# A hand-written order of two cycles for the score matmuls of an attention and Fourier-mixing kernel

## The chip, the cores and the metric

The kernel runs on one core of a Trainium2 chip. The metric is the device time of one execution in microseconds (us), the median of several runs. One further execution was taken with the hardware profiler; its page and its trace are what is read here. The engines are named as the profile names them: PE is TensorE's matmul, PEld its weight load, DVE is VectorE, ACT is ScalarE, POOL is GpSimd, SP is SyncE (here it only issues DMAs).

## The reference

Two token mixers over the same input are blended by a gate. x has 2048 rows of 640; there are 32 heads of 20.

```python
def reference(A_x, A_wqkv, A_wo, B_x, B_dft_seq_re, B_dft_seq_im, B_dft_hid_re, B_dft_hid_im, gate_w):
    def _A_ref(x, wqkv, wo):
        ...
        scores = jnp.einsum("bhqd,bhkd->bhqk", q, k) * (Dh ** -0.5)
        p = _softmax(scores, axis=-1)
        o = jnp.einsum("bhqk,bhkd->bhqd", p, v)
        return (lambda x, *d: x.transpose(*d))(o, 0, 2, 1, 3).reshape(B, S, D) @ wo

    def _B_ref(x, dft_seq_re, dft_seq_im, dft_hid_re, dft_hid_im):
        a = jnp.einsum("bsd,ed->bse", x, dft_hid_re)
        b = jnp.einsum("bsd,ed->bse", x, dft_hid_im)
        y = jnp.einsum("ts,bse->bte", dft_seq_re, a) - jnp.einsum("ts,bse->bte", dft_seq_im, b)
        return y

    x = A_x
    g = _sigmoid((x * gate_w).sum(-1, keepdims=True))
    a = _A_ref(x, A_wqkv, A_wo)
    b = _B_ref(x, B_dft_seq_re, B_dft_seq_im, B_dft_hid_re, B_dft_hid_im)
    return g * a + (1 - g) * b
```

## The kernel before

**The stages.** First come the projections: q and k for all heads (stored to DRAM as a high and a low part), v, the gate and the first ten tiles of the DFT along the hidden axis. The long middle is one loop over 1024 steps, in which attention and the rest of the DFT share PE. Then the attention output is multiplied by wo and added to the DFT's result. The middle lasts from about 274 to 1936 us of the profiled execution, and the change lies in it.

**Attention in steps.** A unit is a pair of heads and half of the queries: 32 units of 32 steps. In a step `i` of unit `n`, the scores of 128 keys and 512 queries are computed for each of the two heads, one head from partitions 0 on (the upper half of the PE array, rows 0 to 63), the other from partition 64 on (the lower half). Each is one matmul (line 638) into a PSUM bank, and ACT takes the exponential from that bank into half of the tile `p` (line 641, "the exponential"). The softmax's maximum is not computed on the fly: it is found beforehand, by a second set of score matmuls with queries and keys exchanged (line 151), from whose banks DVE reduces the maximum (line 153). These "maxima" run LEAD = 41 steps ahead of the exponentials. When a unit's maxima are done, `s_end` reduces them to one per query (line 159) and `max_chain` transposes them on PE into a bank (line 179), splits them in two parts on DVE and has SP write them as two extra rows of q, with four DMAs. So the later exponential's matmul has 62 rows and subtracts the maximum by itself.

**Banks.** Score matmuls of both kinds and the transpose take their PSUM bank from `bank()` (line 104), which goes round five banks. So a score can start only when the score five before it has been read, by ACT if it was an exponential's, by DVE if it was a maximum's. Two more banks (`yp0`, `yp1`) belong to the DFT, one (`av`) to the product with v.

**A cycle of four steps.** A step issues, by `mixed(0)` and `mixed(1)`, an exponential's matmul of one head and a maximum's matmul of the other, so that both halves of the array work at once. After each pair comes a place for DFT work, `fill(i, z)`. A fill is one `next(fills)`: a pair of matmuls with 320 columns, one for each half (line 510; line 287 in the hidden stage). At the end of each fourth step, the last place is taken by a burst instead (line 651): `run_extras` (reads of finished DFT tiles by ACT and DVE, `finish_y` on DVE, and POOL's preparations), and `av_step` for two key tiles, 8 matmul calls of 512 columns (line 435; the profile shows 16 instructions), which use the whole array. With e for an exponential's matmul, m for a maximum's, F for a place for fills and B for the burst, a cycle is

```
em F em F em F em F em F em F em F em B
```

eight e, eight m, seven places. The 54 first cycles carry the rest of the hidden DFT, one tile of 15 fills each. From the 58th on come the 56 units of the sequence DFT, 48 fills each, spread over three or four cycles (lines 601 to 609), which makes 16 or 12 fills in a cycle. The last ten cycles have no maxima left.

**The step's other work.** `later` holds functions by the step at which they are to be issued (DMAs of SP and POOL for the next heads, for statistics, stores); the loop runs them at the start of each step. `now[0]` is the current step. The tiles `p` have five buffers; a burst frees those of four steps.

Of the kernel before, what the change touches and what calls it, by code (L numbers as in the profile page):

```python
# [12 lines left out]
AF = mybir.ActivationFunctionType  # L13
# [5 lines left out]
P = 128  # L19
# [3 lines left out]
DH = 20  # L23
ND = D // P
NS = S // P
NP = H // 2
HE = D // 2
VW = 2 * (DH + 1)
KROWS = 3 * DH
NU = 2 * NP  # L30
BW = HE + 2
LEAD = 41
HEAD = 10

# [16 lines left out]
def f32(ap):  # L51
    return ap.bitcast(F32)
# [3 lines left out]
def mix_kernel(ctx: ExitStack, tc: tile.TileContext, xa, wqk, wb, cdft, wo, out):  # L56
    nc = tc.nc
    pe, act, dve, pool, sp = nc.tensor, nc.scalar, nc.vector, nc.gpsimd, nc.sync
    ctx.enter_context(tc.manual_schedule())

    def pools(**kw):
        return ctx.enter_context(tc.tile_pool(**kw))
# [19 lines left out]
    kst = [const.tile([P, S], R, name=f"kst{i}") for i in range(2)]  # L82
# [21 lines left out]
    def bank():  # L104
        return ps_w.tile([P, 512], F32, name=f"ps{next(turn) % 5}")

    def pair_tile():
        return work.tile([P, 2, 512], F32, name="p", bufs=5)

    def raw_tile():  # L110
        return work.tile([P, 1024], F32, name="raw", bufs=3)
# [7 lines left out]
    def load_stack(p):  # L119
        kt, qt = kst[p % 2], qst[p % 2]  # L120
        u = S // 2
        for t, o, two, one, cs in ((kt, D, 0, 2, slice(0, S)), (qt, 0, 1, 0, slice(0, u)), (qt, 0, 1, 0, slice(u, S))):
            for h in range(2):
                r = (2 * p + h) * DH
                b = 64 * h
                rows = slice(o + r, o + r + DH)
                yield f32(t[b + two * DH : b + (two + 2) * DH, cs]), qk_scr[:, rows, cs]
                yield f32(t[b + one * DH : b + (one + 1) * DH, cs]), qk_scr[0, rows, cs]

    def q_unit(n):  # L130
        u = n % 2 * (S // 2)
        return qst[n // 2 % 2][:, u : u + S // 2]

    mx, nms = {}, {}
    now, later = [-1], {}

    def at_step(i, fn):
        later.setdefault(i, []).append(fn)


    def s_mm(i, h):
        n, s = divmod(i, 32)
        if n >= NU:
            return lambda: None
        qt, kc = divmod(s, 4)
        q, k = q_unit(n), kst[(n // 2) % 2]
        if n not in mx:
            mx[n] = small.tile([P, 2, 8, 4], F32, name="mx", bufs=2)
        ps = bank()
        b = 64 * h  # L150
        pe.matmul(ps, q[b : b + KROWS, qt * P : (qt + 1) * P],  # L151
                  k[b : b + KROWS, kc * 512 : (kc + 1) * 512], start=True, stop=True)
        return lambda: dve.tensor_reduce(mx[n][:, h, qt, kc : kc + 1], ps, axis=AX.X, op=ALU.max)  # L153

    def s_end(i):
        n, s = divmod(i, 32)
        if n < NU and s == 31:
            nms[n] = small.tile([P, 16], F32, name="nm", bufs=2)
            dve.tensor_reduce(nms[n], mx.pop(n).rearrange("p h q c -> p (h q) c"), axis=AX.X, op=ALU.max, negate=True)
        if s == 1 and 0 < n <= NU:  # L160
            max_chain(n - 1)
# [14 lines left out]
    def max_chain(n):  # L176
        q = q_unit(n)
        pt = bank()[:16, :P]
        pe.transpose(pt, nms.pop(n), ident)
        m1 = small.tile([16, P], R, name="m1", bufs=2)  # L180
        m2 = small.tile([16, P], R, name="m2", bufs=2)
        split(m1, m2, pt, dve, dve)

        def rows():
            for h in range(2):
                b = 64 * h + KROWS
                sp.dma_start(f32(q[b : b + 1, :]), f32(m1[8 * h : 8 * h + 8, :]))
                sp.dma_start(f32(q[b + 1 : b + 2, :]), f32(m2[8 * h : 8 * h + 8, :]))

        if now[0] < 0:  # L190
            rows()
        else:
            at_step(now[0] + 2, rows)
# [27 lines left out]
    def load_wb(j, e1=act, e2=dve):  # L221
        raws = []
        for d in range(0, ND, 3):
            n = min(3, ND - d)
            raw = raw_tile()[:, : n * BW].rearrange("p (d c) -> p d c", d=n)
            sp.dma_start(raw, wb[j, :, d : d + n])
            raws.append((d, n, raw))

        def finish():
            w = proj.tile([P, 2, ND, BW], R, name="wb", bufs=2)  # L230
            for d, n, raw in raws:
                split(w[:, 0, d : d + n], w[:, 1, d : d + n], raw, e1, e2)
            wt["b", j] = w
# [5 lines left out]
    def flush(keep=0):  # L239
        while len(stores) > keep:  # L240
            sp.dma_start(*stores.pop(0))
# [118 lines left out]
    for n, c in enumerate(order):  # L360
        for t in range(4):
            m = 4 * n + t
# [4 lines left out]
            if t == 1:  # L367
                fin()
                if n + 2 < len(order):
                    fin = load_wqk(order[n + 2])  # L370
    run_s(LEAD)
    flush()
# [17 lines left out]
    cparts, vts, pts = {}, {}, {}  # L390
# [38 lines left out]
    def av_step(i, n, kt):  # L429
        v = vts[n // 2]  # L430
        pp = [pts.pop((n, kt, qc)) for qc in range(2)]
        for qc in range(2):
            for h in range(2):
                j = 2 * qc + h
                pe.matmul(av[32 * j : 32 * j + DH + 1, :], v[:, kt, h * (DH + 1) : (h + 1) * (DH + 1)],  # L435
                          pp[qc][:, h, :], start=kt == 0, stop=kt == NS - 1)
        if kt == NS - 1:
            unit_end(i, n)
# [111 lines left out]
    def run_extras(g, most):  # L550
        while extras and most and extras[0][0] <= now[0]:
            extras.pop(0)[1]()
            most -= 1
        if more(g):
            n = g // (HT * NS) + 1
            preps.append(load_a(n, made.setdefault(n, 0)))
            made[n] += 1
        if len(preps) > 2 or preps and not more(g):
            preps.pop(0)()
# [8 lines left out]
    def start_dft():  # L568
        flush()
        proj.release()  # L570
        apool.append(pools(name="apool", bufs=1))
# [13 lines left out]
    total = 32 * NU  # L585
    done = 0
    goals, fins = {}, {}
# [4 lines left out]
    HID = 4 * NS - HEAD  # L592
# [4 lines left out]
    start = 4 * HID  # L597
    HIDS = HID * 3 * ND
# [4 lines left out]
    cycles += [(edge[u], edge[u + 1], 3 * NS) for u in range(UNITS)]  # L603
    at_goal = 0
    for c0, c1, count in cycles:
        slots = [(4 * c + k, z) for c in range(c0, c1) for k in (1, 2, 3, 4) for z in range(2 - k // 4)]
        for f, slot in enumerate(slots):
            goals[slot] = at_goal + count * (f + 1) // len(slots)
        at_goal += count

    def fill(i, z):
        nonlocal done
        while done < goals.get((i, z), 0):
            next(fills)
            done += 1

    for i in range(total + 1):
        now[0] = i
        n, s = divmod(i, 32)
        for fn in later.pop(i, ()):  # L620
            fn()
        if s % 2 == 0:
            flush()
        if i < total:
            kt, qc = divmod(s, 2)
            if s == 0 and n % 2 == 0:
                p = n // 2
                if p + 1 < NP:
                    at_step(i + 6, functools.partial(load_v, p + 1))
                    for j, args in enumerate(load_stack(p + 1)):  # L630
                        at_step(i + 2 + 2 * j, functools.partial(pool.dma_start, *args))
            q, k = q_unit(n), kst[(n // 2) % 2]
            pp = pts[n, kt, qc] = pair_tile()

            def mixed(h):
                b = 64 * h
                pt = bank()
                pe.matmul(pt, k[b : b + KROWS + 2, kt * P : (kt + 1) * P],  # L638
                          q[b : b + KROWS + 2, qc * 512 : (qc + 1) * 512], start=True, stop=True)
                most = s_mm(i + LEAD, 1 - h)  # L640
                act.activation(pp[:, h], pt, AF.Exp, scale=float(DH) ** -0.5)  # L641
                most()

            mixed(0)
            fill(i, 0)
            mixed(1)
            s_end(i + LEAD)
        if start + 2 <= i < start + 2 + HT:
            for k in range(2):
                at_step(i + 3, load_a(0, 2 * (i - start - 2) + k))  # L650
        if i and i % 4 == 0:
            run_extras(max(done - HIDS, 0) // 3, 2)
            j = i // 2 - 2
            for kt in (j, j + 1):
                av_step(i, kt // NS, kt % NS)
        else:
            fill(i, 1)
        if i % 4 == 2:
            c = i // 4
            if c + HEAD in (NS, 2 * NS):  # L660
                load_wb(3 + (c + HEAD) // NS, pool, pool)()
            if c in (HID - 5, HID - 3):
                load_c((c - HID + 5) // 2)()
            if c == HID + 1:
                cfin.append(load_c(2))
        if i == start:
            start_dft()
        if total - 10 <= i < total - 4 and i % 2 == 0:
            tt = (i - total + 10) // 2
            fins[tt] = load_o(tt)  # L670
        if i == total - 3:
            fins[0]()
    assert done == at_goal
    now[0] = total + 4
    run_extras(2 * NS * UNITS, 99)
# [70 lines left out]
```

## Time and profile before

| | us |
|---|---|
| median of 3 runs | 2012.11 (2010.03 to 2013.65) |
| the profiled execution, its own time | 2012.72 |
| its span, first to last instruction | 2011.0 |
| granted TensorE clock, mean | 0.997 of full |
| middle, first burst to last burst | 281.8 to 1935.7 |

| Group of instructions | count | busy us | mean ns |
|---|---|---|---|
| maximum, DVE line 153 | 2048 | 1262.2 | 683 |
| exponential, ACT line 641 | 2048 | 1122.6 | 598 |
| maxima's score matmul, PE line 151 | 2048 | 926.1 | 460 |
| exponentials' score matmul, PE line 638 | 2048 | 823.9 | 409 |
| DFT fill, PE line 510 | 5376 | 734.0 | 309 |
| product with v, PE line 435 | 4096 | 494.7 | 599 |

A line of the timeline gives the start in us from the span's start, how long the group of like instructions lasted, the engine, the line, the operation, the tiles (out<-in), the shapes and how many there were; in brackets stands how long the engine was idle before it and what ended that. PE's times overlap: a matmul's duration runs from its start to its result, and those of the two halves of the array run side by side. A number such as 529/550/2671 is the shortest, the median and the longest of a group, in ns.

### The profile page before, as it was taken

How to read it: one execution, taken by the hardware profiler on the slowest of the kernel's cores; microseconds unless marked ns; L12 is line 12 of the kernel's file. 1: busy time of each engine (PE TensorE's matmuls, PEld its weight loads, DVE VectorE, ACT ScalarE, POOL GpSimd, SP SyncE). 2: the span in 40 equal slices, each digit the busy share in tenths (PEclk: the TensorE clock that was granted, in tenths of full speed). 3: DMA queues.
4: the chain of work that ended last, by engine and by line, in shares of the span. 5: the costliest groups of instructions: out<-in, count | busy, mean ns of one | idle time of the engine just before them, and what ended most of it. 6: DMA issues, size and time to landing. Idle time of an engine off the chain costs nothing. (4 is left out here: it accounts for less than half of the span.)

```text
span 2011.0 us, 44080 instructions
## 1 busy us (share of the span) xinstructions
PE 1974.8 (98%) x17080; PEld 1397.7 (70%) x17080; DVE 1501.9 (75%) x2516; ACT 1253.3 (62%) x2337; POOL 986.6 (49%) x898
## 2 busy tenths in 40 slices
PE   8999999999999999999999999999999999999999
PEld 7987767666675666666666666666666666666679
DVE  3144568878887888888888888888888888888423
ACT  4221147777776666677666666766766676667751
POOL 1210001111006888556368876974775689576510
PEclk9999999999999999999999999999999999999999
DMA  6653321313125475435266736563555556444345
GB/s 218 168 166 132 128 90 45 83 50 82 35 60 161 143 204 159 118 100 153 93 169 194 207 133 194 175 184 100 165 149 145 163 171 200 131 149 144 95 150 184
DMA packets 196514, 281.05 MB, mean 140 GB/s; under 512 B 73372, under 2 KB 137916, under 8 KB 194384
## 3 DMA queue, kind: packets, MB, share of 16 engines
q1 hardware_dynamic: 158992, 246.20, 39.6%
q0 software_dynamic: 37312, 32.03, 6.4%
q8 instruction: 134, 2.20, 0.5%
q14 instruction: 76, 0.62, 0.1%
HBM read 213.81 MB, written 63.70 MB: 138 GB/s over the span
## 5 line engine op out<-in xcount | busy, mean ns | idle before, releaser
L153 DVE TENSOR_REDUCE mx<-ps 128x1 f32<-128x512 f32 x2048 | 1262.2, 683 | 233.8 <-PE ps L151 230.1
L641 ACT ACTIVATE p<-ps 128x512 f32<-128x512 f32 x2048 | 1122.6, 598 | 446.0 <-PE ps L151 354.6
L151 PE MATMUL ps<-kst,qst 60*128 60x512 f32 x2048 | 926.1, 460 | 8.0 <-ACT p L641 3.7
L638 PE MATMUL ps<-qst,kst 62*128 62x512 f32 x2048 | 823.9, 409 | 9.0 <-DVE mx L153 7.6
L510 PE MATMUL yp<-a,part 64*128 64x320 f32 x5376 | 734.0, 309 | 0.1
L510 PEld LDWEIGHTS yp<-a,part 64*128 64x128 f32 x5376 | 596.6, 187 | 23.9 <-DVE m L530 0.3
L638 PEld LDWEIGHTS ps<-qst,kst 62*128 62x128 f32 x2048 | 376.9, 185 | 235.9 <-DVE mx L153 66.9
L435 PE MATMUL av<-p,v 128*21 128x512 f32 x4096 | 494.7, 599 | 0.1
L151 PEld LDWEIGHTS ps<-kst,qst 60*128 60x128 f32 x2048 | 372.0, 184 | 59.5 <-ACT p L641 27.7
L95 POOL TENSOR_TENSOR part<-raw,part 128x1024 fp32r<-128x1024 f32 x112 | 267.1, 2385 | 9.0
L435 PEld LDWEIGHTS av<-p,v 128*21 128x21 f32 x4096 | 98.8, 100 | 226.8 <-issue 219.8
L287 PE MATMUL yp<-wb,xs 64*128 64x320 f32 x1920 | 238.1, 308 | 0.4 <-ACT raw L295 0.3
L94 POOL CAST part<-raw 128x1024 fp32r<-128x1024 f32 x112 | 116.8, 1043 | 205.2 <-PE yp L510 198.6
L406 POOL TENSOR_TENSOR raw<-raw,raw 128x1024 f32<-128x1024 f32 x78 | 188.3, 2414 | 50.1 <-DMA raw<-in_cdft 39.6
L287 PEld LDWEIGHTS yp<-wb,xs 64*128 64x128 f32 x1920 | 205.7, 187 | 9.1 <-ACT raw L295 0.6
L467 POOL TENSOR_TENSOR o<-o,rb 128x512 f32<-128x512 f32 x32 | 41.6, 1300 | 160.7 <-DMA rb<-r_scr 130.0
L94 POOL CAST wb<-raw 128x966 fp32r<-128x966 f32 (+1 forms) x4 | 3.4, 856 | 229.7 <-PE av L435 195.5
L95 POOL TENSOR_TENSOR a<-araw,a 128x320 fp32r<-128x320 f32 x112 | 98.1, 876 | 9.0
L95 DVE TENSOR_TENSOR p<-ps,p 128x512 fp32r<-128x512 f32 x40 | 27.5, 691 | 94.2 <-ACT p L92 94.2
L98 PE MATMUL ps<-xs,part 128*128 128x512 f32 x200 | 80.7, 403 | 9.1 <-ACT xs L92 7.5
L92 ACT ACTIVATE p<-ps 128x512 fp32r<-128x512 f32 x40 | 23.7, 597 | 101.5 <-PE ps L100 101.5
L420 POOL TENSOR_TENSOR araw<-araw 128x320 f32<-128x320 f32 x80 | 71.4, 892 | 20.4 <-DMA araw<-a_scr 19.9
(67 smaller groups left out, 1339.0 us busy)
## 6 DMA issues: line engine op xcount, KB each, us to landing
raw<-in_cdft SPq DMA_DIRECT2D x192, 512.0 KB
araw<-a_scr SPq DMA_DIRECT2D x192, 160.0 KB
qk_scr<-p SPq DMA_DIRECT2D x40, 512.0 KB
y_scr<-yt SPq DMA_DIRECT2D x96, 160.0 KB
kst<-qk_scr POOLq DMA_DIRECT2D x32, 320.0 KB, 12.2
qst<-qk_scr POOLq DMA_DIRECT2D x64, 160.0 KB, 8.8
a_scr<-raw SPq DMA_DIRECT2D x64, 160.0 KB
yt<-y_scr SPq DMA_DIRECT2D x64, 160.0 KB
```

The lines of the kernel that those rows point to most:

```text
L94: e1.tensor_copy(dst1, src)
L95: e2.tensor_tensor(dst2, src, f32(dst1), op=ALU.subtract)
L98: pe.matmul(ps, st1, mv1, start=first, stop=False)
L151: pe.matmul(ps, q[b : b + KROWS, qt * P : (qt + 1) * P], k[b : b + KROWS, kc * 512 : (kc + 1) * 512], start=True, stop=True)
L153: return lambda: dve.tensor_reduce(mx[n][:, h, qt, kc : kc + 1], ps, axis=AX.X, op=ALU.max)
L287: pe.matmul(yp[h][:, :HE], xs[r, xz, d, cs], w[r, wz, d, :HE], start=d == 0 and z == 0, stop=d == ND - 1 and z == 2)
L406: pool.tensor_tensor(raws[0], raws[0], raws[1], op=ALU.add if PRODUCTS[n][0][1][0] > 0 else ALU.subtract)
L420: pool.tensor_tensor(raws[0], raws[0], raws[1], op=ALU.add if PRODUCTS[n][1][1][0] > 0 else ALU.subtract)
L435: pe.matmul(av[32 * j : 32 * j + DH + 1, :], v[:, kt, h * (DH + 1) : (h + 1) * (DH + 1)], pp[qc][:, h, :], start=kt == 0, stop=kt == NS - 1)
L510: pe.matmul(yp[h][:, :HE], c[r, cz, cs], a[r, az], start=s == 0 and z == 0, stop=s == NS - 1 and z == 2)
L638: pe.matmul(pt, k[b : b + KROWS + 2, kt * P : (kt + 1) * P], q[b : b + KROWS + 2, qc * 512 : (qc + 1) * 512], start=True, stop=True)
L641: act.activation(pp[:, h], pt, AF.Exp, scale=float(DH) ** -0.5)
```

## The change

The loop over steps with its fixed pairs is replaced by a loop over cycles that follows a string. `ORDER` has one string for even and one for odd cycles; each letter issues one score (`e`, `m`), one place of fills (`F`) or the burst (`B`). Four scores (`emme`) are issued ahead of the first cycle. `heads` counts the scores of each kind; `FIRST` says, for each of eight steps, which head (and so which half of the array) comes first. Even cycles have eight e, seven m and eleven places, odd cycles eight e, nine m and seventeen places. A cycle keeps its number of fills; they are spread over its places evenly (`goals`). What a step did besides its scores is in `begin(i)`, before the step's first e, and `end(i)`, after its second; the burst has `run_extras`, `av_step` and `start_dft`. The blank lines that the diff adds are left out here.

```diff
--- before.py
+++ after.py
@@ -29,6 +29,13 @@
 KROWS = 3 * DH
 NU = 2 * NP
 BW = HE + 2
+ORDER = ("emmeFFFFmeFFemFFmeFFemFeemB", "ememmFFFFFeFmFemFFFeeFFmmFFFFFeemmB")
+FIRST = {"e": (1, 1, 1, 0, 0, 1, 1, 0), "m": (0, 0, 0, 0, 0, 0, 0, 1)}
 LEAD = 41
 HEAD = 10
@@ -603,58 +610,39 @@
     cycles += [(edge[u], edge[u + 1], 3 * NS) for u in range(UNITS)]
     at_goal = 0
     for c0, c1, count in cycles:
-        slots = [(4 * c + k, z) for c in range(c0, c1) for k in (1, 2, 3, 4) for z in range(2 - k // 4)]
-        for f, slot in enumerate(slots):
-            goals[slot] = at_goal + count * (f + 1) // len(slots)
-        at_goal += count
-
-    def fill(i, z):
+        for c in range(c0, c1):
+            share = count * (c + 1 - c0) // (c1 - c0) - count * (c - c0) // (c1 - c0)
+            places = ORDER[c % 2].count("F")
+            goals[c] = [at_goal + share * (f + 1) // places for f in range(places)]
+            at_goal += share
+    def fill(c):
         nonlocal done
-        while done < goals.get((i, z), 0):
+        goal = goals[c].pop(0) if c in goals else 0
+        while done < goal:
             next(fills)
             done += 1
-    for i in range(total + 1):
+    def begin(i):
         now[0] = i
         n, s = divmod(i, 32)
         for fn in later.pop(i, ()):
             fn()
         if s % 2 == 0:
             flush()
+        if s == 0 and n % 2 == 0:
+            p = n // 2
+            if p + 1 < NP:
+                at_step(i + 6, functools.partial(load_v, p + 1))
+                for j, args in enumerate(load_stack(p + 1)):
+                    at_step(i + 2 + 2 * j, functools.partial(pool.dma_start, *args))
         if i < total:
-            kt, qc = divmod(s, 2)
-            if s == 0 and n % 2 == 0:
-                p = n // 2
-                if p + 1 < NP:
-                    at_step(i + 6, functools.partial(load_v, p + 1))
-                    for j, args in enumerate(load_stack(p + 1)):
-                        at_step(i + 2 + 2 * j, functools.partial(pool.dma_start, *args))
-            q, k = q_unit(n), kst[(n // 2) % 2]
-            pp = pts[n, kt, qc] = pair_tile()
-
-            def mixed(h):
-                b = 64 * h
-                pt = bank()
-                pe.matmul(pt, k[b : b + KROWS + 2, kt * P : (kt + 1) * P],
-                          q[b : b + KROWS + 2, qc * 512 : (qc + 1) * 512], start=True, stop=True)
-                most = s_mm(i + LEAD, 1 - h)
-                act.activation(pp[:, h], pt, AF.Exp, scale=float(DH) ** -0.5)
-                most()
-
-            mixed(0)
-            fill(i, 0)
-            mixed(1)
-            s_end(i + LEAD)
+            pts[n, s // 2, s % 2] = pair_tile()
+    def end(i):
         if start + 2 <= i < start + 2 + HT:
             for k in range(2):
                 at_step(i + 3, load_a(0, 2 * (i - start - 2) + k))
-        if i and i % 4 == 0:
-            run_extras(max(done - HIDS, 0) // 3, 2)
-            j = i // 2 - 2
-            for kt in (j, j + 1):
-                av_step(i, kt // NS, kt % NS)
-        else:
-            fill(i, 1)
         if i % 4 == 2:
             c = i // 4
             if c + HEAD in (NS, 2 * NS):
@@ -663,13 +651,55 @@
                 load_c((c - HID + 5) // 2)()
             if c == HID + 1:
                 cfin.append(load_c(2))
-        if i == start:
-            start_dft()
         if total - 10 <= i < total - 4 and i % 2 == 0:
             tt = (i - total + 10) // 2
             fins[tt] = load_o(tt)
         if i == total - 3:
             fins[0]()
+    heads = {"e": 0, "m": 2 * LEAD}
+    def score(kind):
+        x = heads[kind]
+        heads[kind] += 1
+        i, z = divmod(x, 2)
+        h = z ^ FIRST[kind][(i - (LEAD if kind == "m" else 0) - 1) % 8]
+        if kind == "m":
+            s_mm(i, h)()
+            if z:
+                s_end(i)
+            return
+        if z == 0 and i <= total:
+            begin(i)
+        if i < total:
+            n, s = divmod(i, 32)
+            kt, qc = divmod(s, 2)
+            q, k = q_unit(n), kst[(n // 2) % 2]
+            b = 64 * h
+            pt = bank()
+            pe.matmul(pt, k[b : b + KROWS + 2, kt * P : (kt + 1) * P],
+                      q[b : b + KROWS + 2, qc * 512 : (qc + 1) * 512], start=True, stop=True)
+            act.activation(pts[n, kt, qc][:, h], pt, AF.Exp, scale=float(DH) ** -0.5)
+            if z:
+                end(i)
+    def burst(c):
+        run_extras(max(done - HIDS, 0) // 3, 2)
+        for kt in (2 * c, 2 * c + 1):
+            av_step(now[0], kt // NS, kt % NS)
+        if c == HID - 1:
+            start_dft()
+    for kind in "emme":
+        score(kind)
+    for c in range(total // 4):
+        for kind in ORDER[c % 2]:
+            if kind == "F":
+                fill(c)
+            elif kind == "B":
+                burst(c)
+            else:
+                score(kind)
     assert done == at_goal
     now[0] = total + 4
     run_extras(2 * NS * UNITS, 99)
```

## The prediction

> **What bounds it now.** I read the page's shares first, then single cycles in the timeline, then who waits for whom. The page:
>
> ```profile
> PE 1974.8 (98%) x17080; PEld 1397.7 (70%) x17080; DVE 1501.9 (75%) x2516; ACT 1253.3 (62%) x2337; POOL 986.6 (49%) x898
> ```
>
> PE's 98% says little, since a matmul that waits behind another counts as busy. One cycle of four steps with 12 fills (timeline, all engines, the lines that matter):
>
> ```profile
> 1600.56 1.91 PE L435 MATMUL av<-p,v 128*21 128x512 f32 x16
> ...
> 1602.41 0.50 PE L638 MATMUL ps<-qst,kst 62*128 62x512 f32 x1
> ...
> 1602.98 4.89 DVE L153 TENSOR_REDUCE mx<-ps 128x1 f32<-128x512 f32 x8 [0.30 <-PE ps L151]
> 1603.01 3.30 ACT L641 ACTIVATE p<-ps 128x512 f32<-128x512 f32 x6 [1.72 <-PE ps L151]
> 1603.13 0.46 PE L510 MATMUL yp<-a,part 64*128 64x320 f32 x4
> ...
> 1603.65 0.18 PEld L151 LDWEIGHTS ps<-kst,qst 60*128 60x128 f32 x1 [0.19 <-ACT p L641]
> ...
> 1605.37 0.18 PEld L151 LDWEIGHTS ps<-kst,qst 60*128 60x128 f32 x1
> ...
> 1606.39 0.19 PEld L151 LDWEIGHTS ps<-kst,qst 60*128 60x128 f32 x1
> ...
> 1606.54 0.40 PE L151 MATMUL ps<-kst,qst 60*128 60x512 f32 x1
> ...
> 1606.86 1.91 PE L435 MATMUL av<-p,v 128*21 128x512 f32 x16
> ```
>
> From burst to burst: 6.30. The burst and the way out of it take 1.85 (1600.56 to 1602.41), the scores and fills 4.45. DVE works without a gap for 4.89 and then idles until the next scores; ACT idles 1.72. What sets the 4.45 is the five banks. Scores alternate e, m, e, m, and each takes the bank of the fifth before it, so the k-th maximum's matmul waits for exponential k-2. The third maximum's load comes at 1603.65, 0.04 after the first exponential (1603.01 + 0.60); the fourth exponential's matmul is queued behind it in its half of the array, its exponential holds back maximum six (load at 1605.37), and so on to the burst. With 16 fills the same reading gives 6.60, a mix of this wait and PE's own work:
>
> ```profile
> 1005.58 1.91 PE L435 MATMUL av<-p,v 128*21 128x512 f32 x16
> ...
> 1012.18 1.91 PE L435 MATMUL av<-p,v 128*21 128x512 f32 x16
> ```
>
> With 15 fills (the hidden stage) it is 6.44, below from 366.36 to 372.80; the cycle before it, in which the statistics of a unit are transposed, took 6.69:
>
> ```profile
> 359.67 1.91 PE L435 MATMUL av<-p,v 128*21 128x512 f32 x16
> ...
> 366.36 1.91 PE L435 MATMUL av<-p,v 128*21 128x512 f32 x16
> 372.80 1.91 PE L435 MATMUL av<-p,v 128*21 128x512 f32 x16
> ```
>
> **The rules of my walk**, all from the first timeline, in us from a cycle's first score. Its result is there at 0.50; the first maximum starts at 0.57 (1602.98 - 1602.41), the first exponential at 0.60. Maxima follow each other by 0.60 ((4.89 - 0.68) / 7, with 0.68 for one) and exponentials by 0.49. Two scores in the two halves of the array run together and take 0.23, a fill 0.15 (1603.13: two fills 0.46, one lasts 0.31). A freed bank lets the load start 0.05 later. If the half is idle by then, the load's 0.11 is exposed and the result comes 0.50 after it, not 0.39. Loads go in program order, so a waiting one also holds what comes behind it in the other half. The burst starts 0.32 after the last score (1606.54 to 1606.86), 0.43 after a late load. With these the old cycle comes out at 4.45 (12 fills) and 4.75 (16), as measured.
>
> **What the change costs, part by part.** No instruction is added or taken away, the score of a step keeps its DMAs, and SP's and POOL's queues get the same items in the same order; a step's DMAs leave when its first exponential is issued. The statistics' four DMAs now go out up to about a microsecond later, but the unit that needs them starts more than one whole cycle (over 6 us) on, against 2 to 3 us of issuing and landing: nothing. Without that cover it would be those 2 to 3 us in each of 31 units. What changes is who holds which bank.
>
> Cycle of nine maxima (e1 m1 e2 m2 m3, fills, e3 m4 e4 m5, fills, e5 e6, fills, m6 m7, fills, e7 e8 m8 m9): by the rule of five, m6 waits for m4 and m9 for m6. Maxima start at 0.57, 1.17, 1.77 and 2.37; the fourth ends at 3.05, m6's load starts at 3.10 and its maximum runs from 3.64 to 4.32, m9's load starts at 4.37, the burst at 4.80. So DVE sets it: **4.80** with 12 fills, though PE could be there by 4.3. With 15 and 16 fills the last loads fall under running matmuls (0.145 from load to matmul, the fills' own spacing), and I get **4.84** and **4.88**. The price of DVE's queue is new here: nine maxima where the old cycle had eight, and the sixth of them is waited for.
>
> Cycle of seven (e1 m1 m2 e2, fills, m3 e3, fills, e4 m4, fills, m5 e5, fills, e6 m6, fill, e7 e8 m7): m4 waits for m2 (load at 1.90), e8 for m5 (maxima 1.77, 2.44, 3.04 to 3.72; load 3.77) and m7 is queued behind e8: burst at **4.24** with 12 fills, **4.29** with 15. With 16, PE itself is last: 0.34 for the first pair, 7 x 0.23 and 16 x 0.147, last load 0.11: **4.40**. The burst needs the exponentials of all but the last step; the last of them ends at about 4.1, and its second half only needs it 0.85 later: no cost.
>
> Two cycles with both bursts (2 x 1.85), new against old: 12 fills 12.74 against 12.60; 15 fills 12.83 against 12.90; 16 fills 12.98 against 13.20. There are 54 hidden cycles, then 56 units over 198 cycles, 30 of four cycles (12 fills each) and 26 of three (16). Without the first, and the last ten, which have no maxima: 56 pairs x 0.14 = +7.8, 26.5 x -0.07 = -1.9, 38.5 x -0.22 = -8.5. Sum **-2.6**.
>
> The transpose (line 179), once per unit, waits for a bank as well:
>
> ```profile
>   PEld ps L179: 10.4, 30
> ```
>
> 0.35 each now. In the new order it always falls behind m9 of a cycle of nine, and its bank is m7's: that maximum ends at 4.92, and at 5.09 after the unit's last reduction (0.22, of which about 0.17 delays the rest). Transpose at 5.14, burst 0.21 later: 5.35, which is 0.55 more than 4.80. The old cycle paid 0.25 (6.69 against 6.44). 30 x 0.30 = **+9**.
>
> The last ten cycles, without maxima, take 4.75 each, set by ACT. The cycle of nine puts its last two exponentials right before the burst, so ACT starts later: 0 to 0.2 each, I take **+1** in all. Late DVE work, see the rivals: **+1**. Sum: -2.6 + 9 + 1 + 1 = +8; against the profiled execution's 2012.7 (span 2011.0 and 1.7 around it), which is 0.6 above the median of the runs, I take **2019 us**: slower by 0.3%. About 0.2%, 4 us, is what a measurement of this kernel can tell from no change.
>
> What the trace does not show is a score alone in its half beside a fill (m3, e3 and m4 in the cycle of nine, m7 in that of seven). At best it hides wholly under the other half's work and a late load costs nothing (-0.11 at two places, -0.07 for DVE's gap at m6): -0.3 per pair. At worst each blocks both halves for a score's 0.23 on top: +0.3 per pair where DVE does not cover it. Over 126 pairs that is 38 us either way. I take zero, as the nearest rows (loads at 1603.65 and 1605.37, with the other half working on) need no extra term.
>
> **Rivals.**
>
> Faster: the irregular time is swallowed. First to last burst is 281.8 to 1929.1, 1647 us; the regular lengths sum to 53 x 6.45 + 3 x 6.3 + 112 x 6.30 + 77 x 6.60 + 10 x 4.75 = 1622. The other 25 us are transposes and vector work that ends after the next scores are ready. In the cycle of seven DVE is done 0.75 after the burst starts (m7's maximum at 4.31 to 4.99) and has 1.67 until the next maximum, against 1.41 now; if that, and PE's slack in the nine, takes up 20 of the 25 and the transposes' +9 does not come, the time is 2013 - 3 - 20 = **1990**. For it: DVE idles longer where a cycle of seven ends. Against: it idles less after nine. Chance 0.35.
>
> Slower: late DVE work after the nine maxima. There the ninth ends at 6.12 and the next maximum is due at 7.22: 1.10 of room, not 1.41. It decides once a burst's late work is longer than 1.10.
>
> ```profile
> L542 DVE SCALAR_TENSOR_TENSOR yt<-m,ngate,yt x64: 529/550/2671, 865.2 to 1934.1; 128x320 f32<-128x320 f32 x64
> ```
>
> Two such sums are often in one burst, and some take up to 2.67 instead of 0.53, so room runs out. The delay goes straight into the cycle of seven, which ends on its fifth maximum. Price: two bursts with late work per unit, half of them after nine, 56 x 0.31 = 17 at most above the forecast: **2036**. For it: the spread of that row. Against: without stretching, two fit (1.06). The Trainium skill, "SBUF — State Buffer", section "Who interferes with whom", says that a VectorE instruction with two SBUF inputs contends with a GpSimd instruction that reads SBUF. The trace agrees: this row reads two SBUF tiles and stretches, while line 530, with one input from PSUM, stays at 468 to 493 ns. Chance 0.2.
>
> No change, because PE lets scores pass the order written down: the loads keep program order in the trace, so little: 0.05, and 2012.
>
> **How the numbers follow.** Forecast 0.4 (2006 to 2032), faster rival 0.35, slower 0.2, none 0.05. Of the forecast's own spread about 0.28 lies above 2016, 0.08 within 4 us of 2012 and 0.04 below. Faster by over 0.2%: 0.04 + 0.33 = 0.37; within 0.08 + 0.02 + 0.03 of "no change" = 0.13; slower 0.28 + 0.2 + 0.02 = 0.50. The range takes in both bounds of the unknown term, and the rivals: 1976 to 2050.
>
> **What would show it.** Bursts alternately about 6.1 to 6.25 and 6.65 to 6.75 apart; in the longer, the last maximum's load 0.05 after the end of the sixth maximum; the transpose's wait at 30 x 0.6 or more; DVE in the longer burst busy to within a microsecond of the next scores. It is wrong if the cycle of nine ends by 4.5 after its first score, or the cycle of seven needs more than 4.5 with 12 fills.

## The result and the profile after

The changed kernel takes 2046.46 us (median of 4 runs, 2045.89 to 2050.50) against 2012.88 for the kernel before beside it: a ratio of 1.0175, interval 1.016 to 1.019. It is slower by 34 us; the forecast of 2019 lies 6 above that kernel. The profiled execution spans 2044.6 us (2011.0 before), so the two traces differ by what the runs differ by.

The page after, with the engines' shares and the groups of maxima and exponentials (instructions, busy us, mean ns, idle time before them):

```profile
PE 1998.8 (98%) x17080; PEld 1376.2 (67%) x17080; DVE 1549.4 (76%) x2516; ACT 1245.6 (61%) x2337; POOL 986.8 (48%) x898
...
L160 DVE TENSOR_REDUCE mx<-ps 128x1 f32<-128x512 f32 x2048 | 1286.9, 682 | 212.2 <-PE ps L158 182.5
L682 ACT ACTIVATE p<-ps 128x512 f32<-128x512 f32 x2048 | 1114.7, 598 | 497.0 <-PE ps L158 274.7
```

The counts are the same and the instructions of these two groups are no longer than before. DVE is busy 47.5 us longer all the same (1501.9 before), so some other work on it has grown. Where it costs time has to be looked for cycle by cycle. Consecutive bursts in the timeline after (the last line has x8 only because the view ends there):

```profile
1649.43 1.91 PE L442 MATMUL av<-p,v 128*21 128x512 f32 x16
...
1655.50 1.92 PE L442 MATMUL av<-p,v 128*21 128x512 f32 x16
1662.16 1.92 PE L442 MATMUL av<-p,v 128*21 128x512 f32 x16
1668.23 1.92 PE L442 MATMUL av<-p,v 128*21 128x512 f32 x16
1675.97 1.06 PE L442 MATMUL av<-p,v 128*21 128x512 f32 x8
```

The cycles take 6.07 (seven maxima, 12 fills), 6.66 (nine), 6.07 (seven), and then 7.74 in a cycle of nine. The first three are what the prediction's walk gave (6.09, 6.65, 6.09). The inside of the cycle from 1655.50 on is the walk's chain, point for point:

```profile
1657.35 0.50 PE L680 MATMUL ps<-qst,kst 62*128 62x512 f32 x1
...
1657.92 4.36 DVE L160 TENSOR_REDUCE mx<-ps 128x1 f32<-128x512 f32 x7 [1.59 <-PE ps L158]
...
1660.45 0.19 PEld L158 LDWEIGHTS ps<-kst,qst 60*128 60x128 f32 x2 [0.23 <-DVE mx L160]
...
1661.67 0.25 PEld L158 LDWEIGHTS ps<-kst,qst 60*128 60x128 f32 x2 [0.24 <-ACT p L682]
```

Counted from 1657.35: first maximum 0.57, load of m6 3.10 behind the fourth maximum, the last pair's loads at 4.32 and, 0.07 later in the records, 4.39. The first of the two waits for an exponential, the second, which decides, starts 0.05 after the end of the sixth maximum. The burst follows at 4.81; the walk had 4.80.

The 7.74 is what the forecast sized wrong. DVE and POOL around that burst:

```profile
1667.66 1.40 DVE L160 TENSOR_REDUCE mx<-ps 128x1 f32<-128x512 f32 x2
1669.54 0.49 DVE L537 TENSOR_TENSOR m<-yp,m 128x320 f32<-128x320 f32 x1 [0.48 <-ACT m L536]
1670.07 1.76 DVE L549 SCALAR_TENSOR_TENSOR yt<-m,ngate,yt 128x320 f32<-128x320 f32 x1
1671.74 4.35 DVE L160 TENSOR_REDUCE mx<-ps 128x1 f32<-128x512 f32 x7
...
1667.98 1.04 POOL L101 CAST part<-raw 128x1024 fp32r<-128x1024 f32 x1 [0.64 <-PE ps L680]
1669.10 2.38 POOL L102 TENSOR_TENSOR part<-raw,part 128x1024 fp32r<-128x1024 f32 x1
```

Line 537 belongs to the read of a finished DFT tile out of PSUM, line 549 is its finish, which multiplies the tile by the gate and adds it to `yt`. Read and first finish now follow each other in one burst. The finish takes 1.76 instead of 0.55, so the first maximum starts at 1671.74. The scores came 1.85 after the burst at 1668.23, so it was due at 1670.65: it is 1.09 late, and 7.74 - 6.66 = 1.08. Over the whole trace the finish of line 549, which reads two tiles, changed its median from 550 to 1267 ns:

```profile
L549 DVE SCALAR_TENSOR_TENSOR yt<-m,ngate,yt x64: 530/1267/2535, 864.8 to 1965.3; 128x320 f32<-128x320 f32 x64
```

Why they share a burst is in the code, in the place of the fills and not in the banks. A read is stamped with `now[0]` and a finish with `now[0] + 1`, and a burst issues what is stamped up to its own step. Before, a cycle's last place of fills came after the fourth step had begun, so the finish had to wait for the next burst. In both new strings the last F stands ahead of the fourth step's first e, so the stamps are one smaller and the finish is let into the same burst. There POOL is at work: the unit's last fill has just freed a tile of DFT matrices, and POOL splits the next into it, by the cast and the subtraction above. The subtraction runs from 1669.10 to 1671.48, all through the time in which a finish of 0.55 would have been done.

### The profile page after: what moved, and what is told of

It is laid out like the page before. It is cut to its first block, busy times and chain, and to the rows that moved or that the text cites. A ratio compares the mean times of both kernels' runs of the same rounds, so it can differ in the third digit from the quotient of the medians.

```text
span 2044.6 us, 43831 instructions
## 1 busy us (share of the span) xinstructions
PE 1998.8 (98%) x17080; PEld 1376.2 (67%) x17080; DVE 1549.4 (76%) x2516; ACT 1245.6 (61%) x2337; POOL 986.8 (48%) x898
## 5 line engine op out<-in xcount | busy, mean ns | idle before, releaser
L160 DVE TENSOR_REDUCE mx<-ps 128x1 f32<-128x512 f32 x2048 | 1286.9, 682 | 212.2 <-PE ps L158 182.5
L158 PE MATMUL ps<-kst,qst 60*128 60x512 f32 x2048 | 728.0, 440 | 20.1 <-DVE mx L160 13.9
L680 PE MATMUL ps<-qst,kst 62*128 62x512 f32 x2048 | 717.1, 432 | 7.5 <-ACT p L682 4.0
L517 PE MATMUL yp<-a,part 64*128 64x320 f32 x5376 | 669.3, 311 | 0.1
L517 PEld LDWEIGHTS yp<-a,part 64*128 64x128 f32 x5376 | 574.3, 186 | 21.3 <-DVE m L537 0.3
L680 PEld LDWEIGHTS ps<-qst,kst 62*128 62x128 f32 x2048 | 317.9, 185 | 268.3 <-issue 139.7
L158 PEld LDWEIGHTS ps<-kst,qst 60*128 60x128 f32 x2048 | 330.5, 185 | 89.2 <-DVE mx L160 59.3
L294 PE MATMUL yp<-wb,xs 64*128 64x320 f32 x1920 | 221.9, 313 | 0.0
L294 PEld LDWEIGHTS yp<-wb,xs 64*128 64x128 f32 x1920 | 199.8, 189 | 8.3
```

The source lines that it names most:

```text
L158: pe.matmul(ps, q[b : b + KROWS, qt * P : (qt + 1) * P], k[b : b + KROWS, kc * 512 : (kc + 1) * 512], start=True, stop=True)
L294: pe.matmul(yp[h][:, :HE], xs[r, xz, d, cs], w[r, wz, d, :HE], start=d == 0 and z == 0, stop=d == ND - 1 and z == 2)
L517: pe.matmul(yp[h][:, :HE], c[r, cz, cs], a[r, az], start=s == 0 and z == 0, stop=s == NS - 1 and z == 2)
L680: pe.matmul(pt, k[b : b + KROWS + 2, kt * P : (kt + 1) * P], q[b : b + KROWS + 2, qc * 512 : (qc + 1) * 512], start=True, stop=True)
```

## The experiments

Two theories were left after this. **Late DVE work:** the stamp put read and finish into one burst. **Room:** the slower rival of the prediction, that the cycle of nine leaves too little time for late work wherever it falls. Behind both stood the question whether the regular cycles are understood at all.

**e1, the finish one step later.** The changed kernel with

```diff
-                extras.append((now[0] + 1, functools.partial(finish_y, out_, t, m, y)))
+                extras.append((now[0] + 2, functools.partial(finish_y, out_, t, m, y)))
```

> Theory (late DVE work): in the changed kernel a DFT unit's last fill is issued one step earlier than before, so its read (line 537) and its first finish (lines 549, 551) are allowed in the same burst, where POOL is busy at the same time; those bursts lose 0.5 (after seven maxima) or 1.0 us (after nine). With the finish allowed one step later it falls into the next burst, as before the change. Regular cycles stay at 6.07 to 6.28 and 6.66, about 27 us of irregular time go: 2019 us (2014 to 2024). Rival (room): the cycle of nine leaves DVE only 1.10 us before the next scores and spills wherever the finish lands: 2035 to 2042 us.

Measured: 2022.27 us, ratio to the kernel before 1.0043 (1.0026 to 1.0059). 24 of the 34 us are gone, and the finish is short again:

```profile
L549 DVE SCALAR_TENSOR_TENSOR yt<-m,ngate,yt x64: 530/546/2676, 869.3 to 1944.5; 128x320 f32<-128x320 f32 x64
```

The regular cycles stay at 6.06, 6.14 and 6.27 with seven maxima and 6.66 with nine. In the traces, the cycles with finishes are 42 us over the regular length of their kind in the changed kernel, 12 in e1 and 11 in the kernel before. The theory of late work holds; room does not explain it, as the cycle of nine is the same as in the changed kernel.

**e2, the old order with the finish in the burst of the read:** `now[0] + 1` becomes `now[0]` in the kernel before.

> The old order, with the first finish allowed in the burst of its unit's read. Theory (late DVE work): the room of 1.41 us lies between the changed kernel's 1.67 and 1.10, so about 0.75 us in each of some 55 bursts, less what finishes cost now: 2032 to 2044 us. Rival (room after nine maxima is what matters): with no cycle of nine nothing happens, 2010 to 2018 us.

Measured: 2035.41 us, 1.011 (1.009 to 1.0129). The finish is stretched as in the changed kernel:

```profile
L542 DVE SCALAR_TENSOR_TENSOR yt<-m,ngate,yt x64: 532/953/3637, 864.1 to 1954.2; 128x320 f32<-128x320 f32 x64
```

About the same, 23 us, appears in a kernel that has no cycle of nine, with regular cycles of 6.30, 6.46 and 6.61 as before. So this part of the loss has nothing to do with seven and nine.

**e8 and e9, POOL writes zeros in place of the subtraction.** The low part of the DFT matrices is then left out of the result. In the changed kernel (e8) and the one before (e9):

```diff
-            split(c[:, 0], c[:, 1], raws[0], pool, pool)
+            pool.tensor_copy(c[:, 0], raws[0])
+            pool.memset(f32(c[:, 1]), 0.0)
```

> The changed kernel, but POOL writes zeros for the low part of the sequence DFT's matrices (a memset, which reads nothing) instead of subtracting two tiles in SBUF (2.38 us); the low part is left out of the result. Theory (POOL's reads stretch the finishes): the finishes in the burst of the read shrink from 1.27 us (median) towards 0.55, and most of the 28 us that they cost goes: 2018 to 2028 us. Rival (read and finish in one burst are too much by themselves, with ACT's copy ahead of them): 2040 us or more.

> The kernel before with the same edit. Theory (POOL's reads): only the few stretched finishes of the second burst are to be gained, some 5 us: 2004 to 2010 us, so that e8 stands 10 to 20 us above it (the transposes' 9, the reciprocal's 3, the finishes' place). Rival (the memset frees POOL and PE gains throughout): 1995 us or less.

Measured: e8 2027.61 us, 1.0074 (1.0049 to 1.0098); e9 2001.43 us, 0.9943 (0.9928 to 0.9958). In e8 the median of the finish falls to its short time, although the first finish still shares the burst with the read:

```profile
L550 DVE SCALAR_TENSOR_TENSOR yt<-m,ngate,yt x64: 529/552/2530, 862.8 to 1946.9; 128x320 f32<-128x320 f32 x64
```

So POOL's subtraction had stretched a good part of them, and the read ahead of them had not; 19 us go with it. The traces tell the two apart as well. In the changed kernel 53 cycles begin with a read and a finish in one burst, the last ten cycles left aside. Ten of these finishes take less than 0.6 us, and their cycles are at most 0.01 over the regular length; the 43 others lose 40 us together. In e8 it is 22 without loss, and 31 that lose 26 us. Sharing the burst costs nothing as long as the finish is short.

Whether it is POOL's reading that counts or only how long POOL is busy, the totals do not tell: the memset takes 0.95 each instead of 2.38, and 28 of the 64 finishes of line 550 run while POOL computes nothing, against 16 in the changed kernel. The Trainium skill, "SBUF — State Buffer", section "Who interferes with whom", has it that such a VectorE instruction contends with GpSimd instructions that read SBUF, not with those that only write. The few cases in the traces agree: two finishes ran beside a memset alone in e8, with 542 and 543 ns, and three in e9, with 544 to 552, while the 14 beside the subtraction alone in the changed kernel took 802 to 2501. The longest in e8 are still 2.5 us, next to POOL's other additions of two tiles (2.41).

My expectation for e9 was missed: 11 to 13 us were gained, not 5. The cycles with finishes gained about what was expected (11 us over their regular length before, 5 in e9); where the rest of the gain comes from is not shown. And e8 stands 26 us above e9, not 10 to 20: its 31 long finishes still lose 26 us, against the 5 in e9.

**e3, eight and eight.** As e1, with the maximum that opened the cycle of nine put at the end of the cycle of seven:

```diff
-ORDER = ("emmeFFFFmeFFemFFmeFFemFeemB", "ememmFFFFFeFmFemFFFeeFFmmFFFFFeemmB")
-FIRST = {"e": (1, 1, 1, 0, 0, 1, 1, 0), "m": (0, 0, 0, 0, 0, 0, 0, 1)}
+ORDER = ("emmeFFFFmeFFemFFmeFFemFeemmB", "eemmFFFFFeFmFemFFFeeFFmmFFFFFeemmB")
+FIRST = {"e": (0, 1, 1, 0, 0, 1, 1, 0), "m": (1, 0, 0, 0, 1, 0, 0, 0)}
```

> As e1, but the last maximum's score of the cycle of seven comes one place earlier, before the burst instead of after it with the cycle of nine: eight and eight, everything else in the same order. Theory (banks decide, seven and nine are about even with the old order): the walk gives 6.49 and 6.36 with 12 fills, 6.53 and 6.43 with 15, 6.66 and 6.55 with 16, which is 21 us over e1: 2035 to 2045 us. Rival (nine maxima in one cycle are the harm): shorter than e1, 2010 us or less.

Measured: 2035.17 us, 1.0115 (1.0083 to 1.0147), 13 over e1 instead of 21. The cycles take 6.51 and 6.42 with 12 fills, 6.55 and 6.40 with 15, 6.69 and 6.49 with 16: the walk had 6.49 and 6.36, 6.53 and 6.43, 6.66 and 6.55. What the expectation left out is that transposes and reciprocals come cheaper in this order: 0.40 and nothing over a regular cycle, against 0.55 and 0.11 in e1, which is 8 us in all. Seven and nine in themselves are not the harm; even numbers with the same neighbours are worse.

**e4, an order found with the walk.** One string for all cycles:

```diff
-ORDER = ("emmeFFFFmeFFemFFmeFFemFeemB", "ememmFFFFFeFmFemFFFeeFFmmFFFFFeemmB")
-FIRST = {"e": (1, 1, 1, 0, 0, 1, 1, 0), "m": (0, 0, 0, 0, 0, 0, 0, 1)}
+ORDER = ("emFFFmeFFemFeFmeFFemFFFmmeFemB",) * 2
+FIRST = {"e": (0, 0, 1, 1) * 2, "m": (1, 1, 1, 0) * 2}
...
-    for kind in "emme":
+    for kind in "emem":
```

> One order of eight and eight for every cycle (em FFF me FF em F e F me FF em FFF m me F em B), chosen by the walk's rules so that few scores wait for their bank. Theory (the banks' waits set the regular cycle): 6.09, 6.28 and 6.34 with 12, 15 and 16 fills against 6.30, 6.46 and 6.60, 47 us less; the transpose waits longer (+9), the reciprocal (+3) and the finishes find 1.1 us of room (+10): 1987 us (1970 to 2005). Rival (something else than the banks sets the cycle): not below 2010 us.

Measured: 1987.83 us, 0.9888 (0.9856 to 0.9920): faster than both kernels. Two bursts with 12 fills between them:

```profile
1584.47 1.91 PE L442 MATMUL av<-p,v 128*21 128x512 f32 x16
1590.56 1.92 PE L442 MATMUL av<-p,v 128*21 128x512 f32 x16
```

That is 6.09 as walked; with 15 and 16 fills it is 6.25 and 6.38 (walked 6.28 and 6.34). The rules of the banks are thus enough to place scores by. That the total came out at the 1987 expected is in part luck: in the profiled execution, which at 1998.79 is 11 us above the median, the cycles with finishes lose 35 us over their regular length, 24 more than before the change and not 10. This string's last F comes after the fourth step's first e, so its finishes fall into the next burst, as before the change.

**e5, e6, e7: late work apart, and the transpose inside the burst.** e5 is e4 with `run_extras(..., 1)`, one read or finish per burst. e6 is e5, e7 is e1, each with the transpose of a unit's maxima held back until the burst's first key tile is issued:

```diff
-            max_chain(n - 1)
+            held.append(n - 1)
...
             av_step(now[0], kt // NS, kt % NS)
+            if held:
+                max_chain(held.pop())
```

> e4 with one read or finish per burst instead of two. Theory (late DVE work): in e4 two finishes in one burst overrun the 1.1 us of room; apart they fit unless stretched by POOL: about 10 us less than e4, 1974 to 1983 us. Rival (each finish is stretched by POOL on its own, so that it is all the same how they are spread): as e4, 1985 to 1992 us.

> e5 with the transpose of the maxima issued between the burst's two key tiles instead of ahead of the burst. Theory (the transpose waits for its bank): the bank is free by then, only the transpose's own 0.28 us stays of about 0.5: 30 x 0.25 = 7 us less than e5, 1967 to 1976 us. Rival (the price is that of switching the array to it): as e5 or longer.

> e1 (the change with the finish one step later) with the transpose in the burst as in e6. Theory (bank): the 7.21 us cycles fall to about 6.66 + 0.28, 30 x 0.27 = 8 us less than e1: 2011 to 2017 us, no more than 0.2% from the kernel before. Rival (switching): as e1, 2019 to 2025 us.

Measured: e5 1981.10 us, 0.9849 (0.9822 to 0.9875), which overlaps with e4, so the gain of one finish per burst is not settled. e6 1982.44, 0.9853 (0.9826 to 0.9880), the same as e5; e7 2022.60, 1.0052 (1.0035 to 1.0070), the same as e1. Both gave nothing where 7 and 8 us were expected. The bursts of e7 around a transpose tell why (the view ends in the last line's burst):

```profile
1623.42 1.92 PE L444 MATMUL av<-p,v 128*21 128x512 f32 x16
1629.49 1.91 PE L444 MATMUL av<-p,v 128*21 128x512 f32 x16
1636.32 1.06 PE L444 MATMUL av<-p,v 128*21 128x512 f32 x8
1637.52 1.06 PE L444 MATMUL av<-p,v 128*21 128x512 f32 x8
1642.72 1.06 PE L444 MATMUL av<-p,v 128*21 128x512 f32 x8
```

The cycle with the unit's reduction falls from 7.21 to 6.83, but the burst, now in two halves of eight, is longer, and the next cycle takes 6.40 instead of 6.07. Of the 0.55 by which a transpose lengthens its cycle, 0.17 are the reduction on DVE and 0.33 the transpose's own time on PE, which only moved; about 0.05 was wait that could be saved. The rival was right about the price.

## Why the prediction was right or wrong

**The number.** 2046 lies within the stated range of 1976 to 2050, but 27 us above the forecast and 10 above the slower rival, the highest time that the prediction argues for. The range was wider than that for a score alone in its half of the array, which cost nothing. That the time lies inside is luck.

**What bounds the kernel, and the walk: right.** Every regular cycle came out within 0.07 of its value: 6.07, 6.15 and 6.27 for seven maxima (6.09, 6.14 and 6.25 forecast), 6.66 for nine at any number of fills (6.65 to 6.73). With the measured lengths, the pairs of cycles sum to 56 x 0.14 - 26.5 x 0.11 - 38.5 x 0.27 = -5 us, where -2.6 was forecast. The term that the trace of before did not show, a score alone in its half, needs nothing on top, as taken.

**The transpose: right in size, wrong in its cause.** Cycles with it take 7.20 to 7.21, 0.55 over 6.66, and cost +9 over before as forecast:

```profile
1587.00 1.91 PE L442 MATMUL av<-p,v 128*21 128x512 f32 x16
...
1594.00 0.28 PE L186 MATMUL ps<-ident,nm 128*16 128x128 f32 x1
1594.20 1.92 PE L442 MATMUL av<-p,v 128*21 128x512 f32 x16
```

But e7 shows that most of it was its own time and DVE's, not the wait for m7's bank that I gave as the reason. The sign that I named for that wait, 30 x 0.6 or more, did not come either: the load of the transpose waited 12.3 us in 30, 0.41 each, against 0.35 before.

**"Late DVE work, see the rivals: +1": this is the step that failed.** e1 measures it at 24 us. The +1 had no working of its own. The sentence that what changes is who holds which bank left out that a place of fills moved ahead of the beginning of a step, and that work stamped with that step moved with it, into the burst in which POOL splits matrices. I counted the instructions that each step issues and not what is stamped by the step in which a fill is issued.

**A small term was missing.** A unit's reciprocal on DVE falls into the cycle of nine, which DVE sets: 6.77 instead of 6.66 once per eight cycles, 31 x 0.11 = 3 us, which the old cycle hid (6.29 with and without it).

**The rivals.** The slower one had the right mechanism, finishes stretched beside POOL that run past the room at the burst, and its room after nine maxima, 1.10, is what the trace has (1.08 behind the burst at 1662.16). Its place was wrong, as bursts after seven maxima lose even more (25 us in the 25 cycles of nine behind them, against 15 us in 28 cycles of seven behind a burst after nine), and its price of 17 us was too small, since the finishes also became longer. The faster one did not come, and not in e1 either, where the late work is short again and the cycles with finishes lose as much as before.

**The sums.** The sum that the runs bear out is -5 + 9 + 3 + 24 = 31 of the 34 us. The trace of the changed kernel puts 30 on the finishes instead of 24 (42 against 11) and has 3 to 4 saved elsewhere, which no run explains; in e1's trace, two cycles of the hidden DFT take 6 us more than in the changed kernel. Two slips in the prediction's arithmetic changed little: +8 on a median of 2012.1 is 2020, not 2019; and the stretch up to 1929.1 ends at the last burst but one and has nine cycles of 4.75, not ten, so that its regular lengths sum to 1617 and 30 us are irregular, not 25.

## What to carry to other kernels

When scores or fills change places, follow what is keyed to a step counter, not only the instructions that are moved: here a stamp that was one smaller cost 24 us, where the regular cycles changed by 5. A cycle in which engines hand a few banks round can be worked out from four or five rows (result, reader's time, release, load), closely enough to choose an order by it; such an order gave 1.1% here. An instruction moved out of a wait gains only the wait: take its own time off the price first, as e6 and e7 show.

## What the hardware showed

In these traces a DVE instruction that runs beside POOL's work can be recorded as a long one, with no idle time before it: 0.53 to 2.5 us for the same form (line 549), while line 537, with one input from PSUM, stays at 468 to 493 ns beside the same subtraction. Two input tiles are not a condition: the finish that writes a tile for the first time reads only one (line 551) and was stretched as well, with a median of 712 ns against 412 before and 1.38 to 1.74 us for the five that ran beside the subtraction alone.

The score matmuls of the two halves of the array do not always start in the order in which they are written. In the kernel before, a maximum's matmul whose exponential comes first in the program starts up to 0.20 us ahead of it, as line 151 at 1005.06 and line 638 at 1005.25. In the middle of the changed kernel neighbouring scores keep their order to within 0.03.
